# Attention with two heads at once on the halves of the matrix array, and unsplit 4-byte products

## The chip, the cores and the metric

One core of a Trainium2 chip runs the whole program. The metric is the device time of one execution in microseconds. The engines have short names in the profile: PE is the matrix engine (PEld its weight loads), DVE the vector engine, ACT the scalar engine, POOL GpSimd, and SP the engine whose queue issues nearly all DMA transfers.

## The reference

The program computes attention with a learned bias, then a layer of three products joined by a maximum, then a gated sum over eight experts. Batch 2, 8 heads, 576 positions, head size 64. All inputs are 4-byte floats, and the results must be as exact as 4-byte arithmetic nearly allows.

```
scores = q k^T / sqrt(64) + bias          # bias: small network of log distances, one value per (i, j, head)
attn   = softmax(scores);  a = attn v     # a: [2, 8, 576, 64]
x = a as [1152, 512]                      # heads side by side
h = max(x w1, x w2, x w3);  x = h w_out   # [1152, 768], [1152, 512]
P = eight rounds of row and column scaling of exp(x w_gate)
out = sum over e of P[:, e] * (relu(x w1[e]) w2[e])
```

Only the attention line is touched by the change.

## The kernel before

The program runs in stages: the bias table (0 to 68.5 us in the profiled execution), attention (68.5 to some 209), the three-product layer (to 357) and the experts (the rest). [...] Tiles come from pools with a fixed number of buffers, and an instruction that needs a buffer waits for the last reader of the buffer's former content.

The matrix engine multiplies in a reduced 4-byte format (F32R). To get nearly full precision, operands are split into a high part (a rounded copy) and a low part (what is left). For queries, the high part stands in partitions 0 to 63 and the low part in 64 to 127 (`qs`), so one product with the keys' high part (doubled over both halves) and one with their low part give the whole. `prep_head` makes these parts for one head on GpSimd (for the first head partly on ACT, inside the bias stage), and `load_head` brings the next head's raw data.

The unit of attention is one head, one batch and 128 queries: 9 units a head (the ninth holds the last 64 queries of both batches), 72 units in all. The loop at L684 runs over steps `s`. In step `s` the matrix engine does the scores of unit `s` (`u_qk`, L482), the transposes of an earlier unit's probabilities (`u_tr`, L556, and `u_trl`, L565, for the last 64 keys), and a part of the products with the values of an earlier unit (`pv_mm`, L608, by the table `PV`). DVE adds the bias and takes the negated maximum (`u_max`, L499), ACT takes the exponential with its sum (`u_exp`, L510). `split` (L569, L570) evicts the transposed block twice: ACT writes the high part and DVE the low part. `pv_ev` joins the two halves of the value product's result. The row sums' reciprocals go to DRAM and come back as a broadcast (`r_out`, `r_in`); `x_out` on GpSimd scales a pair of heads and splits it into `xh` and `xl`, the operands of the next layer.

Bias rows for later units are loaded by `load_bias` on SP's queue, four units ahead. `w_step` does one small piece of the preparation of the next layer's weights wherever the loop calls it. After the last unit the loop runs 18 more steps for what is left; `m1_first` puts twelve groups of three products of the next layer there (L658).

The gate logits (L1118) and the gate's small transposes (L1127) belong to the experts' stage; they are not changed, and are mentioned since they use the array in parts or with few columns.

Of the kernel before, what the change touches and what calls it, by code (L numbers as in the profile page):

```python
# [27 lines left out]
SH = S // 2  # L28
# [8 lines left out]
W_AT = (0, 3, 6)  # L37
NEARLY = (3, 3, 0, 0, 3, 0, 3)
LASTV = 2
NW2 = 0  # L40
# [14 lines left out]
def make_body(stop=None):  # L55
    def body(tc, a):
# [21 lines left out]
        with ctx, tc.manual_schedule():  # L78
# [4 lines left out]
            r_d = dram.tile([H, 9, 128], F32, name="r_d")  # L83
# [89 lines left out]
            qs = [hp_.tile([128, B, 640], F32R, name=f"qs{p}", bufs=1) for p in range(2)]  # L173
            kt = [[hp_.tile([128, B, S], F32R, name=f"k{x}{p}", bufs=1) for x in "hl"] for p in range(2)]
            vs = [hp_.tile([128, B, 5, 128], F32R, name=f"vs{p}", bufs=1) for p in range(2)]
            for p in range(2):
                G.memset(raw(qs[p][:, 0, 576:640]), 0.0)
            raw_t = {}
            bias_t = {}

            def load_head(h, part=None):
                if h < H:
                    if not part:
                        raw_t[h] = (hp_.tile([128, 2, B, S], F32, tag="qk", name="qk"),
                                    hp_.tile([128, B, 5, D], F32, tag="vr", name="vr"))
                    qk, vr = raw_t[h]
                    if part is None:
                        dma(qk, a["qk"][h])
                    elif part < 2:
                        dma(qk[:, part], a["qk"][h][:, part])  # L190
                    if part in (None, 2):
                        dma(vr, a["v"][h])

            def prep_head(h, step, b=None, on_act=False):

                p = h % 2
                qk, vr = raw_t[h]
                bs = slice(0, B) if b is None else slice(b, b + 1)
                if step[0] == "q":
                    rows = slice(0, 128) if step[1] == "h" else slice(64, 128)  # L200
                    out = hi = qs[p][rows, bs, 0:S]
                    src = qk[rows, 0, bs]
                elif step[0] == "k":
                    out, hi = kt[p]["hl".index(step[1])][:, bs], kt[p][0][:, bs]
                    src = qk[:, 1, bs]
                else:
                    m = lambda x: x.rearrange("p b j d -> p (b j) d")
                    oh = 64 * (h % 2)
                    ol = 64 - oh
                    v = m(vs[p][:, bs])  # L210
                    hi = v[:, :, oh:oh + D]
                    out = hi if step[1] == "h" else v[:, :, ol:ol + D]
                    src = m(vr[:, bs])
                if step[1] == "l":
                    G.tensor_tensor(out=out, in0=src, in1=raw(hi), op=ALU.subtract)
                elif on_act:
                    A.activation(out=out, in_=src, func=AF.Copy)
                else:
                    pool_copy(out, src)

            def load_bias(m):
                h, it = divmod(m, 5)
                t = hp_.tile([128, S], F32, tag="bias", name="bias", bufs=4)
                if it < 4:
                    dma(t, bias_d[128 * it:128 * it + 128, h, :])
                else:
                    for e in range(2):
                        dma(t[64 * e:64 * e + 64], bias_d[512:576, h, :])
                bias_t[h, it] = t


            with ExitStack() as bctx:
# [10 lines left out]
                load_head(0)  # L243
# [116 lines left out]
                for step in ("qh", "kh"):  # L360
                    prep_head(0, step, on_act=True)
                pieces = [("ql", 0), ("ql", 1), ("kl", 0), ("kl", 1), ("vh", None, True)]
# [56 lines left out]
                for g16 in range(NG16):  # L419
                    ps = bias_mm(g16)  # L420
                    t = bias_ev(g16, ps)
                    for c in range(4):
                        if g16 + 2 < NG16:
                            gen_s(4 * (g16 + 2) + c)
                    bias_out(g16, ps, t)
                    if g16 == NG16 - 1:

                        A.activation(out=bc.tile([128, 1], F32, name="ex"), in_=ones[:, 0:1], func=AF.Exp)
                    for n in range(max(g16 - 1, 0), NG16 if g16 == NG16 - 1 else g16):
                        bias_store(n)  # L430
                    if g16 in (12, 20, 28, 35):
                        load_bias((12, 20, 28, 35).index(g16))
                    if g16 in (3, 5, 7):
                        load_head(1, (3, 5, 7).index(g16))
                    if g16 % 4 == 3 and 7 < g16 < 28:
                        prep_head(0, *pieces.pop(0))
# [18 lines left out]
            with ExitStack() as actx:  # L455
                pt_p = actx.enter_context(pool("pt"))
                up = actx.enter_context(pool("up", bufs=2))
                ps_t = actx.enter_context(pool("ps_t", bufs=2, space=PSUM))
                ps_l = actx.enter_context(pool("ps_l", bufs=1, space=PSUM))
                ps_v = actx.enter_context(pool("ps_v", bufs=1, space=PSUM))  # L460
# [4 lines left out]
                pth = [pt_p.tile([128, 5, 2 * w], F32R, name=f"pth{w}") for w in CW]  # L465
                ptl = [pt_p.tile([128, 4, 2 * w], F32R, name=f"ptl{w}") for w in CW]
                un = {}

                def u_qk(u):
                    h, k = divmod(u, 9)  # L470
                    sc = ps_s.tile([128, 2, 512], F32, tag="sc", name="sc")
                    if k < 8:
                        b, it = k % 2, k // 2
                        mm = [(b, 704 * b + 128 * it)]
                    else:
                        mm = [(0, 512), (1, 576)]
                    q = qs[h % 2].rearrange("p b c -> p (b c)")
                    for hf in range(2):
                        y = 0
                        for b, c0 in mm:  # L480
                            for x in kt[h % 2]:
                                T.matmul(out=sc[:, hf, :SH], lhsT=q[:, c0:c0 + 128],  # L482
                                         rhs=x[:, b, hf * SH:hf * SH + SH],
                                         start=(y == 0), stop=(y == 2 * len(mm) - 1))
                                y += 1
                    un[u] = {"sc": sc}
# [4 lines left out]
                def u_max(u):  # L491
                    h, k = divmod(u, 9)
                    w = un[u]
                    ng = up.tile([128, S], F32, tag="ng", name="ng", bufs=3)
                    if k == 0:

                        st_t[h] = up.tile([128, 2, 9], F32, tag="st", name="st", bufs=3)
                    c = U_COL[k]
                    V.tensor_tensor_reduce(  # L499
                        out=ng.rearrange("p (f n) -> p f n", f=2), in0=w["sc"][:, :, :SH],  # L500
                        in1=bias_t[h, k // 2].rearrange("p (f n) -> p f n", f=2),
# [902 lines left out]
```

## Time and profile before

| | |
|---|---|
| median of 3 runs | 1076.7 us (1075.28 to 1077.46) |
| the profiled execution | 1075.73 us, its span 1073.9 us |
| mean granted clock of the matrix engine | 0.992 of full speed |
| busy share of the span: DVE, ACT, POOL | 74%, 55%, 37% |

The span runs from the first to the last instruction; the execution's own time holds 1.8 us more. A line of a group reads: line, engine, operation, tile written and tiles read, shape, how many, then busy time, mean duration of one, and the idle time of the engine before it with what ended it. Shapes such as `128*64 128x128` are rows and columns of the array in use, then partitions and moving columns. Durations of products hold the array's latency; how often one starts is read from a timeline, where like neighbours are merged (`x4` with one start and the time to the end of the last).

### The profile page before, as it was taken

Reading aid. Unit: us, or ns where it says so; the run is one execution under the profiler, and the core shown is the slowest. Engines: PE = TensorE matmul, PEld = TensorE weight load, DVE = VectorE, ACT = ScalarE, POOL = GpSimd, SP = SyncE. Lnnn points to the kernel's source line nnn. Section 1 sums busy time; section 2 is a strip of 40 time slices with the busy share of each in tenths; the row PEclk is TensorE's granted clock in tenths of the full one; section 3 lists DMA queues with packets and bytes.
Section 4 is the critical chain, followed back from the end, with each engine's and each line's share of the span. In section 5 each row is a group of like instructions: output and inputs, shape, how many; then the busy total and the mean of one; then the engine's idle time right before and its main releaser. Section 6 shows DMA issues by size and latency. Waiting matters only on the chain.

```text
span 1073.9 us, 18476 instructions
## 1 busy us (share of the span) xinstructions
PE 1042.3 (97%) x7145; PEld 732.6 (68%) x7145; DVE 796.4 (74%) x1548; ACT 593.0 (55%) x1003; POOL 401.8 (37%) x284
## 2 busy tenths in 40 slices
PE   7779999999999899999999999999999999999998
PEld 3259988999999765664755746657566575664753
DVE  8999999799967776967667677666775666757543
ACT  7989988544425566444545444545445454544530
POOL 6996998122215224135132231331413314123120
PEclk8999999999999999999999999999999999999999
DMA  5878765244522012123021130211302212010002
GB/s 189 277 235 271 224 193 135 64 156 118 121 82 77 21 59 68 23 62 82 22 64 31 54 84 21 64 45 40 84 20 65 64 26 78 22 44 6 1 1 89
DMA packets 41063, 90.78 MB, mean 85 GB/s; under 512 B 8264, under 2 KB 11280, under 8 KB 40080
## 3 DMA queue, kind: packets, MB, share of 16 engines
q1 hardware_dynamic: 40832, 89.31, 28.8%
q8 instruction: 56, 0.92, 0.4%
q10 hardware_dynamic: 144, 0.29, 0.1%
q14 instruction: 31, 0.25, 0.1%
HBM read 75.50 MB, written 13.30 MB: 83 GB/s over the span
## 4 chain that ended last, share of the span: by engine, by line
PE 81%; DVE 11%; ACT 3%; POOL 3%; issue 2%; DMA 0%; DVEq 0%; ACTq 0%; POOLq 0%
PE d L1307 33%; PE x L1222 11%; PE m L658 10%; PE y L1222 8%; PE z L1222 8%; PE sc L482 3%; PE pv L608 2%; POOL s L356 2%; PE pt L556 2%; DVE ng L499 1%; PE p L381 1%; DVE ptl L570 1%; PE o L1073 1%; DVE s L1236 1%; DVE hl L1245 1%
## 5 line engine op out<-in xcount | busy, mean ns | idle before, releaser
L1307 PE MATMUL d<-w2h,hh 128*128 128x512 f16 x576 | 218.3, 379 | 0.7 <-DVE acc L1318 0.7
L1307 PE MATMUL d<-w2h,hl 128*128 128x512 f16 x576 | 218.3, 379 | 0.2 <-DVE hl L1245 0.2
L1307 PE MATMUL d<-w2l,hh 128*128 128x512 f16 x576 | 218.3, 379 | 0.0
L1222 PEld LDWEIGHTS <-w1h 128*128 128x128 f16 x1792 | 175.3, 98 | 49.8 <-issue 2.4
L1307 PEld LDWEIGHTS <-hh 128*128 128x128 f16 x1152 | 112.6, 98 | 132.9 <-issue 1.0
L953 POOL TENSOR_TENSOR w1l<-wf,w1h 128x768 f16<-128x768 f32 x32 | 53.6, 1675 | 359.7 <-ACT w1h L952 285.5
L1321 DVE SCALAR_TENSOR_TENSOR acc<-d,kh,acc 128x512 f32<-128x512 f32 x126 | 94.3, 748 | 93.8 <-PE d L1307 93.6
L1240 ACT ACTIVATE hh<-s 128x576 f16<-128x576 f32 x128 | 87.3, 683 | 128.5 <-DVE s L1236 100.9
L1245 DVE SCALAR_TENSOR_TENSOR hl<-s,hh 128x576 f16<-128x576 f32 x128 | 99.2, 776 | 47.4 <-ACT hh L1240 44.9
L959 POOL TENSOR_TENSOR w1l<-wf,w1h 128x1024 f16<-128x1024 f32 x32 | 68.8, 2151 | 117.6 <-ACT w1h L956 117.6
L956 ACT ACTIVATE w1h<-wf 128x1024 f16<-128x1024 f32 x32 | 33.8, 1055 | 132.5 <-DVE wf L949 132.5
L1222 PEld LDWEIGHTS <-w1l 128*128 128x128 f16 x896 | 87.9, 98 | 22.7 <-issue 0.4
L1307 PEld LDWEIGHTS <-hl 128*128 128x128 f16 x576 | 56.4, 98 | 68.5 <-DVE hl L1245 0.7
L1232 ACT ACTIVATE s<-x,cx 128x576 f32<-128x576 f32 x96 | 70.2, 732 | 28.6 <-PE x L1222 26.9
L1034 POOL TENSOR_TENSOR w2l<-w2r,w2h 128x512 f16<-128x512 f32 x64 | 73.1, 1161 | 25.1 <-ACT w2h L1033 25.1
L1222 PE MATMUL x<-xth,w1h 128*128 128x288 f16 x384 | 78.5, 286 | 0.8 <-ACT s L1232 0.8
L1222 PE MATMUL x<-xtl,w1h 128*128 128x288 f16 x384 | 78.6, 286 | 0.2 <-POOL xtl L964 0.2
L1222 PE MATMUL x<-xth,w1l 128*128 128x288 f16 x384 | 78.5, 286 | 0.0
L1236 DVE SCALAR_TENSOR_TENSOR s<-z,cx,s 128x576 f32<-128x576 f32 x64 | 52.3, 817 | 32.1 <-PE z L1222 25.6
L658 PE MATMUL m<-xl,wh 128*128 128x384 f32 x216 | 72.5, 336 | 0.0
L658 PE MATMUL m<-xh,wh 128*128 128x384 f32 x216 | 72.4, 335 | 0.0
L658 PE MATMUL m<-xh,wl 128*128 128x384 f32 x216 | 72.4, 335 | 0.0
(226 smaller groups left out, 2335.7 us busy)
## 6 DMA issues: line engine op xcount, KB each, us to landing
wr<-in_moe_w SPq DMA_DIRECT2D x50, 512.0 KB, 3.7
w2r<-in_moe_w SPq DMA_DIRECT2D x64, 256.0 KB, 3.0
bias_f<-bo SPq DMA_DIRECT2D x36, 295.5 KB, 3.6
bias<-bias_f SPq DMA_DIRECT2D x32, 288.0 KB, 2.8
qk<-in_qk SPq DMA_DIRECT2D x7, 1152.0 KB, 6.3
wr<-in_moe_w_out SPq DMA_DIRECT2D x6, 512.0 KB, 5.4
vr<-in_v SPq DMA_DIRECT2D x8, 320.0 KB, 6.9
bias<-bias_f SPq DMA_DIRECT2D x16, 144.0 KB, 6.3
```

Source lines behind the costliest of these rows:

```text
L658: T.matmul(out=p[:, :TG], lhsT=ws[:, 128 * c:128 * c + 128], rhs=xs[:, c, TG * g:TG * g + TG], start=(c == 0 and n == 0), stop=(c == 3 and ...
L953: G.tensor_tensor(out=lo[:, 0:3], in0=t[:, 1:4], in1=hi[:, 0:3], op=ALU.subtract)
L956: A.activation(out=hi[:, 3:7], in_=t[:, 4:8], func=AF.Copy)
L959: G.tensor_tensor(out=lo[:, 3:7], in0=t[:, 4:8], in1=hi[:, 3:7], op=ALU.subtract)
L1034: G.tensor_tensor(out=lo, in0=r, in1=hi, op=ALU.subtract)
L1222: T.matmul(out=ps[bank][:, s, :SH], lhsT=ws[:, i, c, :], rhs=xv[:, j, c, s * SH:s * SH + SH], start=(start and k == 0), stop=(k == 5), **kw)
L1232: A.activation(out=t, in_=src, func=AF.Identity, scale=c)
L1236: V.scalar_tensor_tensor(out=out, in0=z, scalar=scale, in1=out, op0=ALU.mult, op1=ALU.add)
L1240: A.activation(out=o, in_=src, func=AF.Relu)
L1245: V.scalar_tensor_tensor(out=l, in0=src, scalar=0.0, in1=o, op0=ALU.max, op1=ALU.subtract)
L1307: T.matmul(out=pd, lhsT=hs[:, fh, 128 * t:128 * t + 128], rhs=ws, start=(k == 0), stop=(k == 11))
L1321: V.scalar_tensor_tensor(out=acc[:, t, :], in0=pd, scalar=kh[:, 1 + t:2 + t], in1=acc[:, t, :], op0=ALU.mult, op1=ALU.add)
```

## The change

Scores, transposes and value products use 4-byte floats unsplit; the splits of `q`, `k` and `v` are gone, and the host lays out two heads in partitions 0 to 63 and 64 to 127. One step of the loop now does two heads of the same batch and queries (36 steps). The probabilities are transposed in halves of 64 queries into one buffer of two banks, five blocks of keys each (the fifth starts at key 448, and the values have zeros for its first 64 keys). ACT copies the first head's block, DVE the second's. The value products put the two heads into the two column halves of the array. Row sums of two heads are handled together. What followed the loop is written out.

```
+W_AT = (0, 2, 4, 5, 7)
+            def load_pair(p):
+                if p < H // 2:
+                    qk_t[p] = hp_.tile([128, 2, B, S], F32, tag="qk", name="qk")
+                    v_t[p] = hp_.tile([128, 2, B, 5, D], F32, tag="v", name="v")
+                    for part in range(2):
+                        dma(qk_t[p][:, part], a["qk"][p][:, part])
+                    dma(v_t[p], a["v"][p])
-                for step in ("qh", "kh"):
-                    prep_head(0, step, on_act=True)
-                    if g16 % 4 == 3 and 7 < g16 < 28:
-                        prep_head(0, *pieces.pop(0))
-                ps_t = actx.enter_context(pool("ps_t", bufs=2, space=PSUM))
-                ps_l = actx.enter_context(pool("ps_l", bufs=1, space=PSUM))
-                ps_v = actx.enter_context(pool("ps_v", bufs=1, space=PSUM))
+                ps_t = actx.enter_context(pool("ps_t", bufs=1, space=PSUM))
+                ps_v = actx.enter_context(pool("ps_v", bufs=2, space=PSUM))
+                half = (slice(0, 64), slice(64, 128))
                 def u_qk(u):
+                    sc = [ps_s.tile([128, 2, 512], F32, tag="sc", name="sc") for _ in range(2)]
+                    for hf in range(2):
+                        cs = slice(hf * SH, hf * SH + SH)
+                        for x in range(2):
+                            r = half[x]
+                            if k < 8:
+                                b, it = k % 2, k // 2
+                                T.matmul(out=sc[x][:, hf, :SH], lhsT=q[r, b, 128 * it:128 * it + 128], rhs=kk[r, b, cs],
+                                         start=True, stop=True)
+                            else:
+                                for b in range(B):
+                                    T.matmul(out=sc[x][half[b], hf, :SH], lhsT=q[r, b, 512:576], rhs=kk[r, b, cs],
+                                             start=True, stop=True)
+                def u_tr(u, x):
+                    pe = un[u]["pe"][x]
+                    pt = un[u]["pt"] = ps_t.tile([128, 2, 512], F32, tag="pt", name="pt")
+                    for j in range(5):
+                        c = min(128 * j, S - 128)
+                        for i in range(2):
+                            T.transpose(pt[:, i, 64 * j:64 * j + 64], pe[half[i], c:c + 128], ident[half[i], half[i]])
+                def u_ev(u, x):
...
+                    src = un[u]["pt"][:, :, :320].rearrange("p i (j n) -> p j i n", n=64)
+                    if x == 0:
+                        A.activation(out=to, in_=src, func=AF.Copy)
+                    else:
+                        V.tensor_copy(out=to, in_=src)
+                def pv_mm(p, ch, b, js, to=None):
...
+                    for j in js:
+                        for x in range(2):
+                            T.matmul(out=to[half[x]], lhsT=v_t[p][:, x, b, j, :], rhs=pts[ch][:, x, j, b * w:b * w + w],
+                                     start=(j == 0), stop=(j == 4))
+                def pv_ev(p, ch, b=None):
+                    ps = pvs.pop(p)
+                    if ch == 0:
+                        x_t[p] = up.tile([128, B, S], F32, tag="x32", name="x32")
+                        A.activation(out=x_t[p][:, :, 0:256], in_=ps.rearrange("p (b i) -> p b i", b=2), func=AF.Copy)
                     else:
+                        A.activation(out=x_t[p][:, b, 256:576], in_=ps[:, :320], func=AF.Copy)
+                PV = {5: (0, 0, (0, 1)), 6: (0, 0, (2, 3)), 7: (0, 0, (4,), 0, 1, (0,)), 8: (0, 1, (1, 2)), 9: (0, 1, (3, 4)),
+                      10: (1, 0, (0, 1)), 11: (1, 0, (2, 3, 4)), 12: (1, 1, (0, 1)), 13: (1, 1, (2, 3, 4))}
+                EV = {9: (0,), 11: (1, 0), 13: (1, 1)}
+                for s in range(NU):
+                    p, k = divmod(s, 9)
+                    u_qk(s)
+                    if s > 0:
+                        u_tr(s - 1, 0)
+                    pv_part(s)
+                    for x in range(2):
+                        u_max(s, x)
+                    if s > 0:
+                        u_ev(s - 1, 0)
+                    u_exp(s, 0)
+                    for n, e in in_turn(EV, s):
+                        pv_ev(n, *e)
+                    u_exp(s, 1)
+                    if s > 0:
+                        u_tr(s - 1, 1)
+                        u_ev(s - 1, 1)
+                    if s > 8:
...
+                        if k == 1:
+                            r_out(p - 1)
+                        if k == 2:
+                            r_in(p - 1)
+                        if k in (6, 7):
+                            x_out(p - 1, k - 6)
+                        if k in W_AT:
+                            w_step(last=2)
...
+                    if s > 0 and (k == 0 or k % 2 == 0) and 5 * p + k // 2 + 2 < 5 * NP:
+                        load_bias(5 * p + k // 2 + 2)
+                    if k == 1:
+                        load_pair(p + 1)
+                u = NU - 1
+                m1_first(2)
+                u_tr(u, 0)
+                u_ev(u, 0)
+                pv_part(NU)
...
+                r_out(NP - 1)
+                r_in(NP - 1)
+                w_step(4, last=3)
+                m1_first(4)
+                pl2 = ps_t.tile([128, 2, 512], F32, tag="pt", name="pv2")
+                for b in range(B):
+                    pv_mm(NP - 1, 1, b, range(5), pl2[:, b, :320])
+                w_step(4, last=3)
+                m1_first(6)
+                for b in range(B):
+                    x_last(b, pl2[:, b, :320])
```

## Rows read from the trace of the kernel before

**Rows 1.** The page: busy us of each engine, share of the span, instructions.

```profile
PE 1042.3 (97%) x7145; PEld 732.6 (68%) x7145; DVE 796.4 (74%) x1548; ACT 593.0 (55%) x1003; POOL 401.8 (37%) x284
```

**Rows 2.** Busy us by stretch: bounds, length, PE, PEld, DVE, ACT, POOL; clock, DMA.

```profile
20.00:42.00 22.00, 19.51 (x252) 5.40 (x253) 22.00 (x48) 20.07 (x46) 20.91 (x18) 1.00 0.90 282
42.00:62.00 20.00, 12.95 (x236) 6.83 (x232) 18.73 (x39) 18.49 (x41) 20.00 (x15) 0.91 0.77 232
...
68.50:193.70 125.20, 121.34 (x919) 114.98 (x920) 120.07 (x267) 112.25 (x264) 101.06 (x67) 0.99 0.68 206
```

**Rows 3.** Timeline of PE, the ends of the attention stage: start, us, instruction, how many.

```profile
68.51 0.61 PE L482 MATMUL sc<-kh,qs 128*128 128x288 f32 x1 [1.68 <-DVE t L390]
...
69.16 0.44 PE L482 MATMUL sc<-kh,qs 128*128 128x288 f32 x1
...
207.14 0.34 PE L658 MATMUL m<-xh,wh 128*128 128x384 f32 x1
...
208.70 0.34 PE L658 MATMUL m<-xh,wh 128*128 128x384 f32 x1
```

**Rows 4.** Timeline of PE within a step of the loop.

```profile
119.60 0.29 PE L482 MATMUL sc<-kh,qs 128*128 128x288 f32 x1
119.73 0.29 PE L482 MATMUL sc<-kl,qs 128*128 128x288 f32 x1
...
120.13 0.60 PE L556 MATMUL pt<-ident,pe 128*128 128x128 f32 x4
120.56 0.49 PE L565 MATMUL pl<-ident,pe 128*64 128x128 f32 x3
...
121.04 0.31 PE L608 MATMUL pv<-pth,vs 128*128 128x320 f32 x1
121.19 0.31 PE L608 MATMUL pv<-ptl,vs 128*128 128x320 f32 x1
```

**Rows 5.** Timelines of ACT and of DVE within a step of the loop.

```profile
121.26 0.77 ACT L510 ACTIVATE pe<-ng,st 128x576 f32<-128x576 f32 x1
...
122.14 0.43 ACT L631 ACTIVATE pvt<-pv 64x320 f32<-64x320 f32 x1
...
121.50 0.75 DVE L499 CUSTOM_DVE_ANT_0 ng<-sc,bias 128x576 f32<-128x576 f32 x1
...
122.17 0.69 DVE L570 TENSOR_TENSOR ptl<-pt,pth 128x512 fp32r<-128x512 f32 x1
```

**Rows 6.** Groups of evictions, whole span: count, busy us, mean ns, idle before.

```profile
L570 DVE TENSOR_TENSOR ptl<-pt,pth 128x512 fp32r<-128x512 f32 x72 | 49.3, 684 | 0.6 <-ACT pth L569 0.5
L569 ACT ACTIVATE pth<-pt 128x512 fp32r<-128x512 f32 x72 | 42.7, 593 | 8.2 <-PE pt L556 7.4
...
L632 DVE TENSOR_TENSOR x<-pv,pvt 64x320 f32<-64x320 f32 x16 | 7.7, 484 | 0.5 <-ACT pvt L631 0.2
...
L631 ACT ACTIVATE pvt<-pv 64x320 f32<-64x320 f32 x16 | 6.9, 431 | 1.7 <-PE pv L608 1.4
```

**Rows 7.** Timeline of PE around the gate logits.

```profile
381.29 0.41 PE L1222 MATMUL z<-xth,w1l 128*128 128x288 f16 x2
...
381.63 2.13 PE L1118 MATMUL pl<-acc,wg 128*8 128x288 f32 x32
383.69 0.42 PE L1222 MATMUL x<-xth,w1h 128*128 128x288 f16 x2
```

**Rows 8.** Timeline of PE at the gate's transposes.

```profile
386.74 0.72 PE L1127 MATMUL pg<-ident,lt 8*128 8x8 f32 x9
```

**Rows 9.** Groups of POOL from 0 to 68.5, splits of the keys.

```profile
L215 POOL TENSOR_TENSOR kl<-qk,kh 128x576 fp32r<-128x576 f32 x2 | 2.8, 1418 | 0.0
```

**Rows 10.** SP's issues in the loop, and from the page issue to landing.

```profile
106.69 1.25 SPq L62 DMA_DIRECT2D r<-r_d  x2
...
vr<-in_v SPq DMA_DIRECT2D x8, 320.0 KB, 6.9
```

More of the change, by code (lines that the diff above doesn't have):

```diff
@@ L194, in prep_head @@
[L194 to L229, printed above, removed]
+            qk_t, v_t = {}, {}
+            bias_t = {}
+            def load_pair(p):
[5 more added lines that the diff above has]
+                    dma(v_t[p], a["v"][p])
@@ new lines, in load_bias @@
+            def load_bias(n):
+                p, it = divmod(n, 5)
+                for h in range(2 * p, 2 * p + 2) if n < 5 * H // 2 else ():
+                    t = hp_.tile([128, S], F32, tag="bias", name="bias", bufs=6)
+                    if it < 4:
+                        dma(t, bias_d[128 * it:128 * it + 128, h, :])
+                    else:
+                        for e in range(2):
+                            dma(t[64 * e:64 * e + 64], bias_d[512:576, h, :])
+                    bias_t[h, it] = t
@@ L466, in body @@
-                ptl = [pt_p.tile([128, 4, 2 * w], F32R, name=f"ptl{w}") for w in CW]
+                pts = [pt_p.tile([128, 2, 5, 2 * w], F32, name=f"pt{w}") for w in CW]
+                half = (slice(0, 64), slice(64, 128))
+                NP, NU = H // 2, 9 * H // 2
                 un = {}
                 def u_qk(u):
[L470 to L477, printed above, removed]
-                    for hf in range(2):
[L479 to L486, printed above, removed]
@@ L499, in u_max @@
                     V.tensor_tensor_reduce(
[L500 to L512 removed]
+                        out=ng.rearrange("p (f n) -> p f n", f=2), in0=un[u]["sc"][x][:, :, :SH],
@@ new lines, in u_max, with u_exp @@
+                        in1=bias_t[2 * p + x, k // 2].rearrange("p (f n) -> p f n", f=2),
+                        op0=ALU.add, op1=ALU.min, scale=-0.125, scalar=3.0e38, accum_out=st_t[p][:, 0, c:c + 1])
+                    un[u]["ng", x] = ng
+                def u_exp(u, x):
+                    p, k = divmod(u, 9)
+                    c = 9 * x + U_COL[k]
+                    pe = up.tile([128, S], F32, tag="pe", name="pe", bufs=6)
+                    A.activation(out=pe, in_=un[u].pop(("ng", x)), func=AF.Exp, bias=st_t[p][:, 0, c:c + 1], scale=-1.0,
+                                 accum_out=st_t[p][:, 1, c:c + 1])
+                    un[u]["pe"].append(pe)
@@ L522, in r_inv @@
-                def r_inv(h):
-                    V.reciprocal(out=st_t[h][:, 1, 0:9].rearrange("p (a b) -> p a b", a=3), in_=rt[0][:, 0:12].rearrange("p (a b) -> p a b", a=3)[:, :, :3])
-                def r_tr(h):
-                    if h == H - 1:
-                        to = ps_t.tile([128, 512], F32, tag="pt", name="pt")[0:9, 0:128]
-                    else:
-                        to = pl_t[0][0:9, 256:384]
-                    T.transpose(to, st_t[h][:, 1, 0:9], ident)
-                    st_t[h] = to
@@ new lines, in r_tr, with r_out, r_in @@
+                def r_tr(p):
+                    pvs[p] = ps_v.tile([128, 512], F32, tag="pv", name="pv")
+                    T.transpose(pvs[p][0:18, 384:512], st_t.pop(p)[:, 1, :], ident)
+                def r_out(p):
+                    A.activation(out=rt[0][0:18], in_=pvs[p][0:18, 384:512], func=AF.Copy)
+                    dma(r_d[p], rt[0][0:18])
+                def r_in(p):
+                    r_t[0] = up.tile([128, B, S], F32, tag="r", name="r", bufs=1)
+                    for x in range(2):
+                        dma(r_t[0][half[x], :, 0:512], r_d[p, 9 * x:9 * x + 8, :].rearrange(
+                            "(b t) p -> b (t p)", b=B).unsqueeze(0).to_broadcast([64, B, 512]))
+                        dma(r_t[0][half[x], :, 512:576], r_d[p, 9 * x + 8, :].rearrange(
+                            "(b p) -> b p", b=B).unsqueeze(0).to_broadcast([64, B, 64]))
```

276 lines of the change are left out of this document (61 added, 215 removed).

## The prediction

> **What bounds the kernel now.** The page comes first: the matrix engine is busy for 97% of the span, so nothing gets shorter unless work on it, or a wait of it, goes [rows 1]. The change touches only the attention stage and what prepares it, so I read that stage alone: the first score product starts at 68.51, the last is issued shortly before 193.7, and the first product that needs the whole attention output starts at 208.70 [rows 2, 3]. That is 140.2 us from the first score to the first full projection product. In the 125.2 us of its loop (72 units of one head and 128 queries, so 1.74 us a unit) the matrix engine is busy 121.3, the vector engine 120.1, the scalar engine 112.3 and GpSimd 101.1: four engines near their limit at once [rows 2]. The starts of single products give what the matrix engine must spend [rows 4]: a score product of 288 columns takes 0.13, a transpose 0.11 ((0.60-0.27)/3), a value product of 320 columns 0.15. With four, five and four of them a unit needs about 1.61 of the 1.74 us; the other 8% are waits, since the vector engine (96% busy) is as full. So the stage pays only if both of these shrink.
>
> **The change, part by part.** One step now does two heads; there are 36. I price a step on each engine.
>
> *Unsplit 4-byte products.* The only ones before on a part of the array are the gate logits: 16 products of 288 columns, four at a time in column quarters, come as 32 records in 2.13 us, each 0.41 long [rows 7]. So each product is two records, and a wave of four takes (2.13-0.41)/7 = 0.246 us, which is two streams of 288 columns at full clock (2 x 0.12); a record is 0.17 longer than its streams. So a product is four streams, and parts of the array do run side by side. A step's scores are four products in two halves: two records each, two halves at once, four waves, 0.98 us (before: eight times 0.13 = 1.06). The value products scale by columns: 0.219 a wave at 256 queries and 0.273 at 320; two waves for one key block of both heads, five blocks, two batches: 20 x 0.219 + 20 x 0.273 = 9.84 us a pair of heads, 1.1 a step (before: eight of up to 0.15). If the halves of the rows, which no row of before shows, don't overlap, the scores cost 1.97: that is the upper end. I take 0.98, because the quarters of the columns overlap fully.
>
> *Transposes.* A step has 20 of 64 moving columns instead of 10 of up to 128. The 128-column ones stream 0.11 each, so 64 columns stream about 0.055. The nine small transposes of the gate have 8 moving columns and the same 128 columns of weights; they come every (0.72-0.20)/8 = 0.065 us [rows 8], so there the weight load sets the pace. Ten per head and step cost 0.65 us if the loads of the two halves queue, and 0.32 if they overlap (before: two units of 0.55). I take 0.32, as for the streams: in the logits four records run together though each has its own weights (of 8 columns only).
>
> *Changes of array shape.* A step goes from row halves to column halves and back. Into the logits the last stream before ends at 381.54 (0.17 ahead of its record) and the first record starts at 381.63; out of them the last stream ends at 383.59 and the next product starts at 383.69 [rows 7]: 0.1 each, 0.2 a step. [...] The row shows less than a record's 0.17 of latency, so I keep 0.1; with 0.17 a step would be 0.14 longer, 5 us over the stage.
>
> *Evictions.* The two splits of each transposed block (scalar copy 0.59, vector subtract 0.68 for 512 columns) become one copy for one head on the scalar engine and one for the other on the vector engine, of 640 columns. From 512 and 320 columns [rows 6] I scale to 0.70 and 0.82. A maximum holds the vector engine 0.67 and an exponential with its sum the scalar engine 0.88 [rows 5]. A step is then 2.16 on the vector engine (before 120.1/36 = 3.3 for two units) and 2.46 on the scalar engine (before 3.1), plus 0.2 to 0.3 for value evictions and weight steps. Neither is first any more.
>
> *What is late next.* The block of transposes has one buffer for both heads. The second head's copy starts 0.2 after the last transpose, runs 0.82 and frees the buffer 1.1 us after the next scores began; these take 0.98, so the first transposes wait 0.12. Behind this waiting instruction stand the value products, since the engine's order is scores, transposes, values, transposes. Both score buffers belong to one step, so the next scores wait for both maxima; in a step with values these are done long before. A step with values costs 0.98+0.12+0.32+0.2+0.32 = 1.94 plus its value products.
>
> *Sum.* 31 steps with values: 31 x 1.94 + 33.1 (four pairs of 9.84, less the 6.3 that stand behind the loop) = 93.2. The first five steps have none and go by the ring of scores and maxima: 0.75 until the first head's scores are streamed, 0.2 until they are seen, two maxima 1.35: 2.3 each, 11.5. The stage starts at the lower clock (records of 0.44 instead of 0.29 [rows 3, 4]): 1.5 more. Behind the loop: twelve early projection groups of three at 0.173 [rows 3], 6.2 as before, value products 6.3, transposes 0.6, changes of shape 0.6: 13.7. Together 119.9. The waits that the loop before has over its plain sum were 8%; I put the same on these 106 us of loop, 8.5.
>
> *The load queue.* A pair's values are loaded into the buffer of the pair before the last, at the pair's step 1, but that buffer is read until step 4. SP works in order, so the queue stands behind this load with the four broadcasts of the row sums, at 0.6 us an issue, and the next bias rows, which are wanted at step 6. Released late in step 4, with 2.8 us of issues ahead and a load of this kind landing 6.9 us after issue [rows 10], the bias can be 2 us late, in two of the four pairs: 3 us, between 0 and 8. That makes 131.4 against 140.2: 8.8 less.
>
> *Before the stage.* Four GpSimd splits of 1.4 us (two of them [rows 9]) and three scalar copies leave the bias stage. GpSimd is busy throughout 42 to 62, but the vector engine has 18.7 of these 20 us itself and all of 20 to 42 [rows 2], so what can come free is at most 1.3, more only if the two get out of each other's way: I take 1, between 0 and 3. GpSimd's other removed work (splits of q, k, v in the loop) hid beside the loop and counts nothing. Nothing behind 208.70 changes.
>
> Together 9.8 us less: 1075.7 (the profiled execution, 1.8 over its span) becomes 1066. The profiled execution lies 1.0 below the median, within the spread of the three times, so I don't correct for it.
>
> **Rivals.**
> 1. *The weight loads of the two halves queue.* Transposes then cost 0.65 twice a step: 0.66 more in 36 steps, 24 us, 1090, slower than before. For it: loads alone set the pace in rows 8, and rows 4 never show two row groups. Against it: the column quarters load side by side. It decides from 0.27 us a step on, where the 9.8 us are used up: a transpose pair at about 0.09 instead of 0.065 is enough.
> 2. *The halves of the rows don't run at once at all.* Then 0.98 more for scores and 0.66 for transposes: 59 us, 1125. For it: no row of before has two row groups in flight. Against it: the logits overlap four column groups without loss.
> [...]
> 4. *The ring holds it.* If each step also waited 0.25 for the single transpose buffer or late bias rows, the gain is gone: 1075. For it: one buffer where there were two, and both score buffers in one step. Against it: by the prices above the vector and scalar engines have 0.3 to 0.8 us spare in each step.
>
> **How the numbers follow.** The forecast has 0.52, with its own range of 1055 to 1073 (waits of 0 to 12%, the queue 0 to 8, the bias stage 0 to 3). Rival 1 has 0.20, rival 2 0.10, rival 3 0.08, rival 4 0.10. This kernel's measurements tell 0.2%, about 2 us, from no change. Faster is the forecast with half of rival 4 and little else, 0.58; within 0.2% 0.05; slower, rivals 1 to 3 without their mildest forms, 0.37. The range of 8 in 10 is 1055 to 1095: it leaves out rival 2 and a rest on the fast side.
>
> **What would show it.** In the changed kernel's timeline score records of both heads start in pairs and a step's scores take about 1.0 (2.0: rival 2); ten transposes take about 0.32 (0.65: rival 1); a step with values takes about 3.2 with the matrix engine nearly always busy; the waits name the vector engine's copy of the transposed block before the first transposes, by about 0.1; and the queue of loads stands between steps 1 and 4 of the second and third pair. Vector and scalar engines should be busy some 70 and 85% of the loop. The first full projection product should start near 199. If it starts later than 208.7, the forecast is wrong, and the duration of the transposes is where I would look first.

## The result

The changed kernel takes 1085.7 us (median of four runs, 1084.35 to 1086.8) against 1076.28 (1075.28 to 1077.46) of the kernel before on the same chip: a ratio of 1.0087 with a 95% interval of 1.0069 to 1.0104. It is slower by 0.9%, where 1066 and faster was forecast; the time lies inside the range, the direction does not. The profiled execution took 1084.35, the lowest of the four, of which 1082.6 are its span.

First the page of the changed kernel, its first part (engine, busy us, share of the span, instructions), which answers to [rows 1]:

```profile
PE 1049.3 (97%) x7533; PEld 686.5 (63%) x7533; DVE 755.8 (70%) x1464; ACT 561.0 (52%) x922; POOL 313.3 (29%) x227
```

The other engines lost work (the vector engine 41 us, GpSimd 88), the matrix engine gained 7. This part of the page doesn't say at what clock. That is seen by stretch: busy us of PE, PEld, DVE, ACT, POOL in the loop of the attention stage, then the granted clock, the share of the DMA engines and GB/s, to be set beside the last line of [rows 2]:

```profile
68.20:202.70 134.50, 120.53 (x1296) 74.43 (x1296) 85.28 (x193) 86.26 (x196) 23.34 (x20) 0.91 0.51 151
```

The clock is the number to see: 0.91 of full speed over the loop, where it was 0.99. And the matrix engine stood for 14 us, with the vector and scalar engines busy for only 63 and 64% of the stretch. So no engine bounds this loop; something makes all of them wait. The ends of the stage, from the timeline of the matrix engine (start, us, instruction, how many), as in [rows 3]:

```profile
68.24 2.24 PE L435 MATMUL sc<-qk 64*128 64x288 f32 x8 [1.77 <-DVE t L349]
...
202.66 0.44 PE L560 MATMUL m<-xh,wh 128*128 128x384 f32 x1
...
216.92 0.34 PE L560 MATMUL m<-xh,wh 128*128 128x384 f32 x1
```

The first score starts 0.27 earlier than before, the first product that needs the whole attention output (216.92) 8.2 later: the stage takes 148.7 us instead of 140.2, and 131.4 were forecast. What lies behind it takes 865.7 of the span, before 865.2. So all is decided between 68.24 and 216.92.

The starts of the score products of successive steps give the length of each step. Steps 0 to 4 take 3.08, 4.96, 3.78, 2.86 and 2.86 us. From step 5 most take 3.0 to 3.1 (value products of 256 queries) or 3.2 to 4.0 (of 320 queries, and more of them). But in the second and in the third pair of heads, steps 6 and 7 take 7.42 and 7.13, and 7.02 and 6.86; in the fourth pair they take 3.0 and 3.1, as they do in all pairs of run 1 below. That is 14.5 and 13.9 where 6.1 would do: 16.2 us lost in two places.

The steady steps look as forecast. Timeline of the matrix engine in two of them, to be set beside [rows 4]:

```profile
115.30 1.19 PE L435 MATMUL sc<-qk 64*128 64x288 f32 x8
116.47 0.53 PE L501 MATMUL pt<-ident,pe 64*128 64x64 f32 x10
116.93 1.08 PE L529 MATMUL pv<-pt,v 128*64 128x256 f32 x8
117.94 0.52 PE L501 MATMUL pt<-ident,pe 64*128 64x64 f32 x10
118.31 1.19 PE L435 MATMUL sc<-qk 64*128 64x288 f32 x8
```

A line here is a run of records and its last record's latency is in it; from start to start the eight score records take 1.17 (a wait for the transposes' buffer is in it), ten transposes 0.46 with the change of shape and 0.37 without, eight value records 1.01 with the change back. The step is 3.01 and has no gap. Its evictions are the copies of L515 and L517 (groups of the stage, as in [rows 6]: count, busy us, mean ns, idle before):

```profile
L517 DVE COPY pt<-pt 128x640 f32<-128x640 f32 x36 | 29.7, 824 | 25.7 <-PE pt L501 25.7
...
L515 ACT ACTIVATE pt<-pt 128x640 f32<-128x640 f32 x36 | 25.4, 705 | 32.5 <-PE pt L501 32.5
```

They take 0.82 and 0.71, as scaled from 512 columns.

**The two places.** The waits of SP's queue in the stage name their source (what waited, for what, us in total, times, longest):

```profile
SPq L59 <- PE pv L529: 15.4, 2, 8.5
```

Twice SP stood up to 8.5 us for value products. What stood behind it is in SP's timeline of the second pair; 106.33 and 115.05 are the loads of q and k and of v of the pair after, in step 1 of this pair:

```profile
105.89 0.34 SPq L59 DMA_DIRECT2D r_d<-rt  x1
106.33 1.67 SPq L59 DMA_DIRECT2D qk<-in_qk  x2
115.05 0.33 SPq L59 DMA_DIRECT2D v<-in_v  x1
115.47 2.57 SPq L59 DMA_DIRECT2D r<-r_d  x4
118.08 12.94 SPq L59 DMA_DIRECT2D bias<-bias_f  x10
```

The load of v was at the head of the queue at 108.0 and went out at 115.05, when the last value product of the pair before had read that buffer (the end of step 4; the scores of step 5 start at 115.30). Then came the four broadcasts of the row sums, and only at 118.08 the bias rows that step 6 wants. Step 6 (scores at 118.31) and step 7 in the timelines of the two engines, the bracket telling the idle time ahead and what ended it:

```profile
118.31 1.19 PE L435 MATMUL sc<-qk 64*128 64x288 f32 x8
...
120.95 0.52 PE L501 MATMUL pt<-ident,pe 64*128 64x64 f32 x10
124.90 0.76 DVE L452 CUSTOM_DVE_ANT_0 ng<-sc,bias 128x576 f32<-128x576 f32 x1 [4.97 <-DMA bias<-bias_f]
125.72 0.75 PE L435 MATMUL sc<-qk 64*128 64x288 f32 x2 [4.25 <-DVE st L452]
127.47 1.80 PE L435 MATMUL sc<-qk 64*128 64x288 f32 x5 [1.00 <-DVE st L452]
...
130.22 1.97 PE L529 MATMUL pv<-pt,v 128*64 128x256 f32 x8
```

The vector engine has the scores and waits 4.97 us for the bias, which lands 6.8 after its issue. The next scores need a buffer that its maxima hold, so the matrix engine stands still for 4.25 and again for 1.00, and the engines lose their overlap: scores, maxima, exponentials and transposes come one after another. And what runs then runs slowly (by stretch, columns as above):

```profile
120.00:125.00 5.00, 1.48 (x19) 0.81 (x18) 0.10 (x1) 0.70 (x1) 1.32 (x1) 1.00 1.06 261
125.00:130.00 5.00, 3.28 (x18) 2.14 (x18) 3.03 (x8) 1.74 (x4) 4.65 (x6) 0.64 0.45 123
130.00:135.00 5.00, 5.00 (x51) 2.79 (x51) 2.71 (x5) 2.53 (x6) 0.96 (x1) 0.68 0.43 120
```

After the idle stretch the granted clock is 0.64 and 0.68 (us by us 1.00 up to 126, 0.50 from 127 to 133, 1.00 again from 134); eight value records take 1.97 instead of 1.08. So 8.4 us are lost in this place, of which 5.0 are the wait for the bias; the other place repeats it (7.8 lost).

### The profile page after: what moved, and what is told of

It is laid out like the page before. It is cut to its first block, busy times and chain, and to the rows that moved or that the text cites. A ratio compares the mean times of both kernels' runs of the same rounds, so it can differ in the third digit from the quotient of the medians.

```text
span 1082.6 us, 18890 instructions
## 1 busy us (share of the span) xinstructions
PE 1049.3 (97%) x7533; PEld 686.5 (63%) x7533; DVE 755.8 (70%) x1464; ACT 561.0 (52%) x922; POOL 313.3 (29%) x227
## 4 chain that ended last, share of the span: by engine, by line
PE 84%; DVE 9%; ACT 3%; DMA 3%; issue 1%; POOL 0%; SPq 0%; DVEq 0%; ACTq 0%
PE d L1211 32%; PE x L1126 12%; PE m L560 10%; PE y L1126 8%; PE z L1126 8%; PE pv L529 3%; PE sc L435 3%; PE pt L501 3%; PE p L340 2%; DVE bo L359 1%; DMA bias<-bias_f 1%; PE o L977 1%; DVE hl L1149 1%; DVE s L1140 1%; DVE pk L704 1%
## 5 line engine op out<-in xcount | busy, mean ns | idle before, releaser
L1211 PEld LDWEIGHTS <-hl 128*128 128x128 f16 x576 | 56.4, 98 | 68.5 <-DVE hl L1149 0.7
```

The costliest lines, as they stand in the source:

```text
L1211: T.matmul(out=pd, lhsT=hs[:, fh, 128 * t:128 * t + 128], rhs=ws, start=(k == 0), stop=(k == 11))
```

## The experiments

The theory: nothing is wrong with the step; the 16.2 us are SP's queue, which stands behind one load. The rivals: the volume of loads in that stretch is the cause and not the order; the lower clock in the first steps is; the step itself is too dear (the halves of the array, the single transpose buffer, the evictions). Runs 1 to 4 shared one chip with each other (kernel before: 1076.34, 15 runs), runs 5 to 8 another (1075.81, 7 runs).

**1. The load of v later.** The values of the third and fourth pair are loaded in step 5 of the pair ahead, when their buffer is free, instead of step 1.

```
-                    dma(v_t[p], a["v"][p])
+                    if p < 2:
+                        dma(v_t[p], a["v"][p])
...
+                    if k == 5 and 0 < p < NP - 1:
+                        dma(v_t[p + 1], a["v"][p + 1])
```

> The values of the third and fourth pair are loaded at step 5 of the pair before, when their buffer is free, instead of at step 1; nothing else changes. Theory (the queue): the load of the values waits in SP's queue for the buffer, the bias rows behind it come 5 us late in the second and third pair, and with the clock that falls meanwhile the two places cost 8.5 and 7.9 us (two steps of 14.5 and 13.9 us instead of 6.0). Then DVE's waits for the bias (10.5 us) vanish, no step behind the first five takes over 4.1 us, and the kernel takes about 1069 us, 16 less than the changed one and 7 less than before. Rival (volume): the 640 KB of values, the broadcasts and the bias rows simply don't fit into these steps; then the bias is late elsewhere and less than a third, 5 us, comes back. Rival (the step): the loss lies in the steps themselves; then no more than 2 us comes back.

Measured: 1065.42 (1065.05 to 1068.32), 0.9904 of the kernel before (0.989 to 0.9917). One load moved turns 0.9% slower into 1% faster. SP's timeline of the same pair, in which the first bias rows now go out at 109.72 instead of 118.08, and v at 115.19:

```profile
104.79 1.44 SPq L59 DMA_DIRECT2D qk<-in_qk  x2
107.05 2.58 SPq L59 DMA_DIRECT2D r<-r_d  x4
109.72 4.89 SPq L59 DMA_DIRECT2D bias<-bias_f  x6
115.19 0.34 SPq L59 DMA_DIRECT2D v<-in_v  x1
```

And step 6 with the step after it on the matrix engine, without a gap:

```profile
116.76 1.19 PE L436 MATMUL sc<-qk 64*128 64x288 f32 x8
...
119.77 1.26 PE L436 MATMUL sc<-qk 64*128 64x288 f32 x8
...
122.88 1.20 PE L440 MATMUL sc<-qk 64*64 64x288 f32 x16
```

3.01 and 3.11 instead of 7.42 and 7.13. The stretch from 125 to 135 is granted the full clock (1.00), so the slow records there followed the idle time. The stage takes 132.1 (first score 66.68, first full product 198.74), where the forecast's sum was 131.4. The theory holds: the steps that took 7.42 and 7.13 are back at their usual length, in both pairs. The time is even 3.6 lower than the 1069 expected, but the traces don't give all of that to the queue: of the 18.6 us between the two profiled executions 16.6 lie in the stage, and 1.6 are an earlier first score (66.68 for 68.24), in a part of the program that is the same in both.

**2. Three buffers for v.** The load stays in its place in SP's order, but finds a free buffer.

```
-                    v_t[p] = hp_.tile([128, 2, B, 5, D], F32, tag="v", name="v")
+                    v_t[p] = hp_.tile([128, 2, B, 5, D], F32, tag="v", name="v", bufs=3)
```

> The values get three buffers instead of two; the load stays at step 1 and in the same place of the queue. Theory (the queue): the wait in SP's queue is gone as in the kernel with the later load, about 1069 us. Rival (volume): with values, broadcasts and bias rows issued within the same three steps the transfers still get into each other's way and the bias rows come late: 1075 or more.

Measured: 1070.42 (1066.89 to 1075.8, ten runs), 0.9947 (0.993 to 0.9965). It is the wait, then, not the amount loaded, that cost most: the same bytes in the same order give 15 of 20 us back. The rest differs from run to run. In the profiled execution (1066.89, the fastest of the ten) the second pair has no gap, and the third a small one:

```profile
148.88 0.52 PE L501 MATMUL pt<-ident,pe 64*128 64x64 f32 x10
150.58 1.67 PE L435 MATMUL sc<-qk 64*128 64x288 f32 x7 [1.17 <-DVE st L452]
```

That the loads sometimes still land late because v is ahead of them would fit, and so would the mean granted clock of the ten, which falls nearly in step as the time grows, from 0.992 in the fastest to 0.982 in the slowest; but it is argued: the slower of the ten have no trace.

**3. The halves' transposes one half after the other.** All five of the first half, then all five of the second, instead of by turns; on the changed kernel.

```
-                    for j in range(5):
-                        c = min(128 * j, S - 128)
-                        for i in range(2):
+                    for i in range(2):
+                        for j in range(5):
+                            c = min(128 * j, S - 128)
```

> Everything as in the changed kernel, but of a head's ten transposes the five of one half of 64 queries are issued first, then the five of the other half, instead of in turn. Theory A (the overlap depends on neighbours in the issue order being on different halves): ten transposes take about 0.62 us instead of 0.31, two times a step: about 0.6 us in each of 31 steps, some 15 to 20 us more, 1101 to 1106. Theory B (the engine finds the other half's work behind five of one half): within 2 us of the changed kernel, 1086.

Measured: 1090.5 (1084.09 to 1092.84), 1.0121 (1.0094 to 1.0149), some 4 to 5 us over the changed kernel by the medians. A steady step takes 3.2 instead of 3.01: neither the full price of no overlap nor none. In the timeline single records of the next group already run among the last of this one:

```profile
141.10 0.58 PE L501 MATMUL pt<-ident,pe 64*128 64x64 f32 x9
141.46 0.46 PE L435 MATMUL sc<-qk 64*128 64x288 f32 x1
141.51 0.23 PE L501 MATMUL pt<-ident,pe 64*128 64x64 f32 x1
141.58 1.19 PE L435 MATMUL sc<-qk 64*128 64x288 f32 x7
142.75 0.61 PE L501 MATMUL pt<-ident,pe 64*128 64x64 f32 x10
143.29 0.28 PE L478 MATMUL pv<-ident,st 128*18 128x128 f32 x1
```

Ten transposes take 0.48 until the scores follow in a row (141.58) and (142.75 to 143.29) 0.54 until a product of the other shape, where by turns it is 0.37 and 0.46. So the halves do run side by side: the engine starts the other half's work before this half's is through, but not from the beginning. How far ahead it looks I didn't measure. The order by turns is worth keeping.

**4. A filling product in the first steps.** A product of 512 columns, whose result nobody reads, after the scores of steps 0 to 3, on the changed kernel: it tells whether the lower clock there costs the time.

```
+                    if s < 4:
+                        fill = ps_v.tile([128, 512], F32, tag="pv", name="fill")
+                        T.matmul(out=fill, lhsT=ident, rhs=qk_t[0][:, 0, 0, :512], start=True, stop=True)
```

> In each of the first four steps one more product of 512 columns (4-byte, full array, its result unused) follows the scores; nothing else changes. Theory (the clock): the engine's idle time in the first steps keeps the clock at its lower level until about 78 us, where before the change it rose at 72, and this costs about 3 us; with the fill it rises at about 72 to 73, steps 2 and 3 (4.96 and 3.78 us) shrink to about 3.2, and the kernel takes 1083 to 1084 us. Rival: these steps are held by the ring through evictions, not by the clock; then the fill costs its own 0.85 to 1.7 us in some of the four steps and the kernel takes 1086 to 1089.

Measured: 1082.05 (1080.29 to 1084.15), 1.0053 (1.0039 to 1.0067). The clock is granted in full from 66 on (1.00 in each stretch of 3 us up to 84), but the first four steps take 14.5 instead of 14.7: the fill stands ahead of the transposes, where it costs what the clock gives. Both bad places are there as before (8.13 and 6.55, 7.46 and 7.10). Neither forecast came true: the steps of 4.96 and 3.78 take 4.53 and 3.87, not 3.2, and the time is below both. So the low clock at the start isn't the main cause of the loss. The 3.7 us gained by the medians are not shown to be the fill's either: of the 2.3 between the two profiled executions none lies in the stage, which takes 148.8 for 148.7; the first score comes 1.2 earlier (67.04 for 68.24), and what lies behind the stage, which is the same program, takes 864.4 for 865.7.

**5. The later load and a fill in an idle place.** Run 1, and in steps 0 to 4 a fill of 384 columns where the value products of later steps stand, between the two groups of transposes.

```
+                    if s < 5:
+                        fill = ps_v.tile([128, 512], F32, tag="pv", name="fill")
+                        T.matmul(out=fill[:, :384], lhsT=ident, rhs=qk_t[0][:, 0, 0, :384], start=True, stop=True)
```

> The kernel with the later load of the values, and in each of the first five steps a product of 384 columns (4-byte, full array, result unused) where later steps have their value products, so between the two blocks of transposes. Theory (the clock): the full-array product after the scores kept the clock at its upper level from 66 us on, but stood ahead of the transposes and cost 0.8 to 1.0 us a step; behind them it lies in the 0.8 us in which the engine waits for the first head's eviction. Then steps 1 to 4 take 2.9 to 3.0 instead of 3.06, 4.96, 3.80 and 2.86, and the kernel takes 1061 to 1063 us against 1065.4. Rival (the ring): the first steps are long for another reason than the clock (transfers of the second pair's data, DVE's waits); then at least one of them stays over 3.5 us and the time stays within 1.5 us of 1065.4.

Measured: 1063.79 (1061.82 to 1065.83), 0.9892 (0.9875 to 0.9908): the lowest median, 1.1% under the kernel before, though its interval overlaps that of run 1. By the medians it gains 1.6 us on run 1, on another chip, between what the theory (2.4 to 4.4) and the rival (up to 1.5) expected; the steps decide between them. By stretch, first the changed kernel, whose matrix engine is idle for 0.9 of the six us, at a granted clock of 0.50:

```profile
72.00:75.00 3.00, 2.82 (x18) 2.40 (x16) 1.33 (x3) 0.99 (x5) 0.00 (x0) 0.50 0.97 378
75.00:78.00 3.00, 2.31 (x18) 1.89 (x20) 1.02 (x3) 2.15 (x5) 0.00 (x0) 0.50 1.00 406
```

and then run 5:

```profile
72.00:75.00 3.00, 2.91 (x31) 1.71 (x30) 1.97 (x6) 2.28 (x6) 0.00 (x0) 1.00 1.02 408
75.00:78.00 3.00, 3.00 (x31) 1.71 (x30) 2.33 (x6) 2.35 (x7) 0.00 (x0) 1.00 1.03 413
```

Steps 0 to 4 take 2.09, 3.45, 2.93, 2.86 and 2.86: 14.2 instead of 17.5. None is over 3.5, though the second stays over the 3.0 expected. So 3.3 us of these steps were the lower clock (0.50 from 69 to 78 in the changed kernel, 1.00 in run 5), and at full clock a step there is still 2.86, not the 2.3 of the forecast.

**6. Each transposed block copied by both engines.** Run 1, with the first 64 queries of every block copied by the scalar engine and the other 64 by the vector engine, so that the single buffer comes free sooner.

```
-                    if x == 0:
-                        A.activation(out=to, in_=src, func=AF.Copy)
-                    else:
-                        V.tensor_copy(out=to, in_=src)
+                    A.activation(out=to[:, :, 0], in_=src[:, :, 0], func=AF.Copy)
+                    V.tensor_copy(out=to[:, :, 1], in_=src[:, :, 1])
```

> The kernel with the later load of the values, but each head's block of transposes is evicted by both engines, the first 64 queries of each 128 by ACT and the rest by DVE, 320 columns each, instead of one head's 640 columns by each engine. Theory (the single buffer): a block then is free 0.4 us earlier, the first transposes of a step no longer wait behind the scores (0.1 us a step) and the ring of the steps without values is 0.7 us shorter: 3 to 6 us less, 1060 to 1062. Rival (the engine's own work sets the step): 3.01 stays 2.95 or more in steps with values, and two more short instructions a step cost ACT and DVE 0.15 us each: 1064 to 1067.

Measured: 1089.45 (1087.81 to 1092.04), 1.0126 (1.0109 to 1.0144): a miss by more than 20 us. Its waits in the stage (who waited for whom, us in total, times, longest):

```profile
PEld pt L502 <- DVE pt L516: 52.9, 67, 2.3
DVE pt L516 <- ACT pt L515: 48.8, 38, 2.1
```

and one step of its timelines:

```profile
137.07 0.53 PE L502 MATMUL pt<-ident,pe 64*128 64x64 f32 x10
...
137.52 0.75 DVE L453 CUSTOM_DVE_ANT_0 ng<-sc,bias 128x576 f32<-128x576 f32 x1
137.63 0.44 ACT L515 ACTIVATE pt<-pt 128x320 f32<-128x320 f32 x1 [1.16 <-PE pt L502]
138.87 0.49 DVE L516 COPY pt<-pt 128x320 f32<-128x320 f32 x1
139.41 0.53 PE L502 MATMUL pt<-ident,pe 64*128 64x64 f32 x10 [0.81 <-DVE pt L516]
```

The copies are shorter (0.44 and 0.49), but the vector engine's part of the first head stands behind both maxima in its order, and the two parts of one tile are done one after the other (the vector engine waited 48.8 us in all for the scalar engine's part): the next transposes start 1.8 after the last ones' end (137.07 and 0.53), where the scalar engine's copy alone takes 0.7. It says nothing on an eviction by two engines in a better order.

**7. Whole transposes.** Run 1, with five transposes of 128 queries on the whole array per head instead of ten of 64: it prices the part of the change that looks dearest, twice as many instructions.

```
-                        for i in range(2):
-                            T.transpose(pt[:, i, 64 * j:64 * j + 64], pe[half[i], c:c + 128], ident[half[i], half[i]])
+                        T.transpose(pt[:, 128 * j:128 * j + 128], pe[:, c:c + 128], ident)
...
-                    src = un[u]["pt"][:, :, :320].rearrange("p i (j n) -> p j i n", n=64)
+                    src = un[u]["pt"].rearrange("p a b -> p (a b)")[:, :640].rearrange("p (j i n) -> p j i n", j=5, i=2)
```

> The kernel with the later load of the values, but the transposes take 128 queries at once on the full array (five of 128 moving columns a head, as before the change) instead of ten of 64 on the two halves. Theory (the halves pay): five cost 0.55 instead of 0.31 us, and the array changes shape four times a step instead of two: 0.7 us more in each of 31 steps, 18 to 24 us, 1084 to 1090. Rival (the evictions hide it): a part of the longer transposes falls into waits, less than 10 us more, under 1075.

Measured: 1084.48 (1081.89 to 1084.85), 1.0073 (1.0058 to 1.0088), so 19 us over run 1 (18 by the ratios to the kernel before, since the chips differ). Its matrix engine:

```profile
146.69 0.77 PE L502 MATMUL pt<-ident,pe 128*128 128x128 f32 x5
147.39 1.24 PE L436 MATMUL sc<-qk 64*128 64x288 f32 x8
148.56 0.77 PE L502 MATMUL pt<-ident,pe 128*128 128x128 f32 x5
149.25 1.30 PE L530 MATMUL pv<-pt,v 128*64 128x320 f32 x8
```

Five whole transposes take 0.69 until the value products and 0.70 (146.69 to 147.39) until the scores, ten halves 0.46 and 0.37. That is 0.56 a step, and the steps are 0.57 longer (3.58 instead of 3.01). Without the 64-query halves the change doesn't pay. The 0.70 holds a change of the array's shape that the halves don't need ahead of scores, some 0.1, an estimate from 0.46 against 0.37; the halves save the rest by working side by side.

**8. Runs 5 and 6 together**, both edits as shown.

> The later load of the values, the fill between the transposes of the first five steps, and evictions of each block by both engines, together. If fill and shared evictions act in different places, their gains add, less what the ring of the first steps has from both: 1057 to 1061. If shared evictions bring nothing: as with the fill alone, 1061 to 1065.

Measured: 1085.28 (1083.43 to 1085.68), 1.0082 (1.0067 to 1.0097). Both expected times are missed by 20 us. The steady steps take 3.49, the same as in run 6, at a mean granted clock of 0.995 in the profiled execution where run 6 has 0.987, so the loss of run 6 is its order, with the two copies behind each other, and not the clock.

## Why the prediction was wrong

The step that failed is **the load queue**. It saw the place, the steps and the chain (SP behind v until late in step 4, four broadcasts, bias rows wanted at step 6) and put 3 us on it, between 0 and 8; measured are 16.2, and moving that load gives all of it back. Two things made it small. First a slip: from the release at 115.05, 2.8 of issues and 6.9 to land [rows 10] end at 124.8 (measured 124.90); the vector engine wanted the bias at 119.9, one step of 3.0 and the scores' 0.75 and its own work behind step 5's start. That is 5 late, by the prices that were on paper, not 2. Second, a late operand was priced at its own lateness: the places lost 8.4 and 7.8, where 5 were waited. The rest is the refilling of a chain across four engines and the lower clock that followed the idle time (0.50 from 127 to 133); I didn't separate these two. The slip alone, 10 us for 3, would have made the forecast 1073, still faster; with 16.2 it would have been 1079, slower. The sign of being wrong was there (216.92, where 208.7 was the limit), but the transposes, where the prediction would have looked first, were nearly as priced (0.37 for 0.32). The time lies inside 1055 to 1095 by luck: the upper end and the 0.37 for slower stood there for rivals 1 to 3, and none of them made it slower.

**The first five steps** were the second miss: 17.5 instead of 13.0. They were priced by scores and maxima, 2.3 each. At full clock (run 5) they take 14.2 together and 2.86 in the steady ones, since the single transpose buffer makes a ring with nothing in it to fill: ten transposes 0.6, the scalar engine's copy 0.7, ten more, then the scores. This is read from the waits (in the changed kernel the second ten transposes of these steps stand 0.8 to 0.9 for that copy); no run gave them a second buffer. That is 2.7 of the miss. The lower clock is the rest, 3.3 where 1.5 were put, since the granted 0.50 lasted to 78 and not to 72 as in the kernel before, whose lines for these stretches are:

```profile
69.00:72.00 3.00, 3.00 (x13) 2.75 (x13) 2.01 (x5) 1.45 (x4) 2.91 (x2) 0.51 0.73 181
72.00:75.00 3.00, 3.00 (x25) 2.73 (x24) 2.69 (x6) 2.39 (x7) 2.92 (x3) 1.00 1.04 311
```

**What was right.** The row halves overlap: a step's scores take 1.17 until the transposes start, for 0.98 and a wait of 0.12, and ten transposes 0.37 before the scores, for 0.32. Rivals 1 and 2 are out. The 0.08 given to rival 3, halves that overlap only in part, rests on no run; in the changed kernel scores and transposes are a tenth over their price (1.05 and twice 0.37 for 0.98 and twice 0.32). The wait is where it was foretold: in the step shown above the vector engine's copy of the block ends at 116.32 and the first transposes start at 116.47 (the view of the waits puts it down to the scalar engine's exponential, which was done by 116.24). Steady steps with values and waits took 100.7 in all for 101.7 forecast (134.4 of loop less 17.5 and 16.2), but this fit is partly luck: 8.5 of the 101.7 were put down for waits, and in run 1, from step 5 to the start of the last step (84.20 to 181.40), the matrix engine has records in all 97.20 us (a wait shorter than a record's latency, some 0.16 by scores of 0.40 that follow each other by 0.24, doesn't show so). What fills the place of the waits are prices a little low: the step of 3.01 was priced at 2.82 (1.94 and four waves of 0.219). The rest came close: the tail behind the loop 14.3 for 13.7; the copies 0.71 and 0.82 for 0.70 and 0.82; nothing behind the stage changed (0.5). The bias stage ended 0.3 earlier for 1; in the variants that share its code the first score starts between 66.68 and 68.31, so one run doesn't tell more than 0.2 to 1.8.

The terms close the account: +13.2 for the queue, +4.5 for the first steps, -1.0 for the steady ones, +0.6 for the tail, +0.7 for the bias stage and +0.5 behind: 18.5 us, from the forecast span of 1064.1 to 1082.6.

**Rival 4**, the ring with late bias rows, came nearest in mechanism, but not as a 0.25 in each step: it was two stalls of 8, and it went past no gain into a loss.

## What to carry to other kernels

When a load is issued by an in-order queue, price it by the moment its buffer is last read, and then price everything behind it in that queue: the operand that comes late may belong to quite another part of the step. Set the landing time beside the time of want on one clock, step by step, and add the refilling of the chain to the wait itself. When a change that is right in its steady step comes out slower, look first at single long steps: here one load moved by four steps separated 0.9% slower from 1% faster.

## What the runs showed of the hardware that was not expected

- Two row halves of the array took 4-byte score products at the same time, with no loss against the column quarters: pairs of score records follow each other by 0.24 (115.60, 115.84 and 116.08 in the step shown above), like the fours of the gate logits by 0.246. Transposes of 64 queries ran side by side too: ten halves need 0.37 where five whole ones need 0.70 with a change of shape of some 0.1 (an estimate, run 7) in it, both ahead of scores. The order of issue mattered: by turns ten take 0.37 until the scores, one half after the other 0.48 (run 3).
- Products of different row halves started out of the program's order: in run 3 the first score record starts at 141.46, the tenth transpose, which stands ahead of it in the program, at 141.51. So it is in step 1 of the changed kernel, where two transposes start at 73.41 and 73.51 and the last score record, which stands ahead of them in the program, at 73.60.
- The granted clock fell after the matrix engine had stood for 4.25 us (1.00 from 120 to 125, 0.64 and 0.68 in the two stretches of 5 us that followed) and was 0.50 from 72 to 78, with idle time in each step; with a fill in each of these steps it was 1.00 there (runs 4 and 5).
